# A scan and an MLP on one NeuronCore: dense idle products, copied states and other queues in the first scan

## The chip, the cores and the metric

The kernel runs on one core of a Trainium2 chip. The time is the device time of one execution in microseconds (us), as a median over runs. The engines are named as in the profile: PE (TensorE; PEld is its weight loading), DVE (VectorE), ACT (ScalarE), POOL (GpSimd) and SP (SyncE, which here only issues DMAs). A "q" after the name of an engine means its queue of DMA issues.

## What is computed

The first part is a state-space scan over 4 batches and 8 heads of 768 steps, in chunks, with state size N = 16 and head size D = 32. The second is an MLP on 3072 tokens with a quick GELU. The scan's output, with its heads side by side, is the MLP's input.

```python
log_a = np.log(np.clip(a, 1e-06, 1.0))
state = zeros((batch, H, N, D))
for c in range(nc):                      # chunks of the sequence
    cum = np.cumsum(la, axis=-1)         # la, xc, Bc, Cc: the chunk's parts
    L = np.exp(cum[:, :, :, None] - cum[:, :, None, :]) * causal
    M = np.einsum('bhin,bhjn->bhij', Cc, Bc) * L
    y_intra = np.einsum('bhij,bhjd->bhid', M, xc)
    y_inter = np.einsum('bhin,bhnd->bhid', Cc, state) * np.exp(cum)[:, :, :, None]
    y[:, :, sl] = y_intra + y_inter
    Bx = np.einsum('bhjn,bhjd->bhjnd', Bc, xc) * decay_from_j
    state = decay_full * state + np.sum(Bx, axis=2)
x = y.transpose(0, 2, 1, 3).reshape(3072, 256)
h = x @ w_in                             # 256 x 2048, float64 weights
out = (h * (1 / (1 + exp(-1.702 * h)))) @ w_out   # 2048 x 256
```

## The kernel before

**Tiling.** The 3072 tokens are cut into six groups of 512 tokens (`NG` groups of `TG`). A group has two pairs (`PG` = 2), a pair has two tiles of 128 tokens, and a tile has two chunks of 64. For each group the scan of its two pairs gives `yT`, the transposed input of the MLP. The MLP has 16 blocks of 128 hidden units; block f needs the weight columns f of `w_in`. Groups 0 and part of group 1 use plain products; in the later ones a product of 2 by 2 blocks is done with seven block products instead of eight (`first` for the hidden layer, `product` for the output).

**Order.** Every engine works through its instructions in the order in which the program's text issues them; `in_order` at the end pins that order. The scan of one group stands in between the products of the group before, so that PE always has products. Group 0 has nothing before it: its scan is the first thing that runs, and PE is then only partly occupied. This first scan is what the change touches.

**The first scan**, by its lines in the profile:

- `rows a` and the logarithm: SP and ACT load `az` (L274), DVE clips it (L339), ACT takes the logarithm (L341), and DVE forms the running sum `cum` inside each chunk (L343).
- `load_first` (L134) loads C and B of group 0 in four DMAs each, `fetch` (L180) loads a piece of the weights, and `load` (L150) loads x (and, for later pairs, b and c) in two DMAs for each of them. Before the change C goes through SP's queue, and B half through ACT's and half through SP's. Then the queue of SP has weight piece 0, x of pairs 0 and 1, and b and c of pair 2.
- `keep_busy` and `pads` (L438, L430) are idle products of PE on a tile of ones; nobody reads what they give. A pad is a product of 32 x 32; `keep_busy` gives products of 192 columns on the whole array.
- `mask_banks` (L546) fills PSUM with the causal mask, `differ_of` (L552) adds the differences of `cum`, and `decay_exp` (L573) takes the exponential on ACT: L.
- `turn_first` (L613) transposes C and B on DVE. `mask_blocks` (L655, ACT) and `mask_first` (L646, POOL) spread a pair's C over its heads. `turn_back` (L625) turns B back on PE for the increments. `score` (L678) multiplies C and B.
- `fields` (L192, L195), `clamp` (L203, L204), `rounded` (L208) and `join` (L219, L225) turn a piece of float64 weights, read as 32-bit words, into float32: `fields`, `rounded` and `join` on DVE, `clamp` on ACT. `narrow(i)` is `rounded(i)`, `fields(i + 1)` and `join(i)`. Pieces 0 to 3 hold two blocks of `w_in` each, pieces 4 and 5 hold four.
- `ends_first` (L466) weights B with the decay to the end of its chunk, `weigh` (L689) multiplies L with the scores, `gain` (L709) gives the increments A of the states, and `since_first` (L510, L515) the decays since a chunk's start.
- `parts_first` (L728) copies A into the tile `steps`, `drops` (L520) sets out the decays, and `keep_first` (L733) runs one scan over `steps`, which leaves the states of all chunks in it. In this tile the elements of one state lie eight elements apart.
- `finish`: `intra` (L814) and `inter` (L802) form y on PE, and two copies (L839, ACT) bring it to `yT`. `table` loads ACT's function table ahead of need. Then come the hidden products of group 0 (L868), first for f = 0.

PSUM has one area of four banks (`area`) which the scores and y take in turn, and four single banks (`bank`) taken in rotation. So y begins when both weighings have read the scores.

`fetch(1, held=True)` writes one word of its tile on DVE, and its DMA waits for that write. In the text it stands behind `weigh(0)`; pieces 2 to 5 and the rest of `a` follow it in SP's queue. After `join(1)` come `fetch(6)` and the load of pair 2's x.

**Later lines.** In group 1 some products are issued in two or four column pieces: `hidden` (L868) and `product` (L1029) cut the first ones, by a number written in the code.

Of the kernel before, what the change touches and what calls it, by code (L numbers as in the profile page):

```python
# [8 lines left out]
FP32 = mybir.dt.float32  # L9
# [7 lines left out]
P = 128  # L17
# [18 lines left out]
def kernel(  # L36
# [31 lines left out]
    nc = tc.nc  # L68
# [17 lines left out]
    R = 4  # L86
# [195 lines left out]
        nc.scalar.activation(early, early, f)  # L282

    table(AF.Ln)
    load_first("C", [nc.sync] * R)
    load_first("B", [nc.scalar] * 2 + [nc.sync] * 2)
    fetch(0)
    load(0, "x")
    load(1, "x")
    load(PG, "bc")  # L290


    edge = const.tile([P, 2], FP32, name="edge")
# [34 lines left out]

    idents = const.tile([P, 2 * NH, H], FP32, name="idents")

    def fold_ident(k):

        nc.vector.tensor_tensor(
            out=idents[:, k * NH:(k + 1) * NH],
            in0=ident[:, :H].unsqueeze(1).to_broadcast([P, NH, H]),
            in1=ident[:, H:].unsqueeze(1).to_broadcast([P, NH, H]), op=ALU.add)
# [393 lines left out]
    def keep_first():  # L730

        flat_steps = steps.rearrange("p e m -> p (e m)")
        nc.vector.tensor_tensor_scan(  # L733
            out=flat_steps, data0=drop.rearrange("p e m -> p (e m)"), data1=flat_steps,
            initial=0.0, op0=ALU.mult, op1=ALU.add)
        for p in range(PG):
            state[p] = steps.rearrange("p e m -> p m e")[:, 4 * p:4 * p + 4]

    def keep_both(pairs):

# [34 lines left out]
    def finish(pairs, steps=range(2)):  # L775


        g, first = divmod(pairs[0], PG)
        early = pairs[0] < PG
        if 0 in steps:  # L780
            begun_y[pairs[0]] = area(f"y{pairs[0]}")[:, :, :len(pairs) * 2 * H].rearrange(
                "p (s t) (k i) -> p s t k i", s=2, i=H), set()
        both, begun = begun_y[pairs[0]]
        y = [both[:, i] for i in range(2)]

        def begin(i, t, parts):
            new = not begun & {(i, t, q) for q in parts}
            begun.update((i, t, q) for q in parts)
            return new

        def inter(n, p, sides=range(2)):

            for k in range(2):
                for i in sides:
                    m = 2 * k + i
                    if (4 * p + m) % (2 * NC) == 0:
                        continue
                    old = state[p][:, m - 1] if m else state[p - 1][:, 3]
                    for r in range(R):
                        t = r // 2  # L800
                        rows, to = slice(32 * r, 32 * r + 32), Q * D * (r % 2)
                        nc.tensor.matmul(  # L802
                            out=y[i][to:to + Q * D, t, 2 * n + k], lhsT=old[rows],
                            rhs=st[p]["CsT"][rows, k, SIDES[i]],
                            start=begin(i, t, range(Q * (r % 2), Q * (r % 2) + Q)), stop=early,
                            tile_position=(32 * r, to), skip_group_check=True)

        def intra(n, p):
            L = Ls[p]
            for k in range(2):  # L810
                for h in range(NH):
                    t, q = divmod(h, HB)
                    for i, side in enumerate(SIDES):
                        nc.tensor.matmul(  # L814
                            out=y[i][D * q:D * q + D, t, 2 * n + k], lhsT=rx[p][side, k, h],
                            rhs=L[side, k, h // Q, h % Q],
                            start=begin(i, t, (q,)), stop=not early, tile_position=(H * i, D * q),
                            skip_group_check=True)

        cols = slice(2 * first * P, 2 * (first + len(pairs)) * P)  # L820

        if first == 0:
            yT[g] = ffn.tile([P, NK, TG], FP32, tag="yT", name=f"yT{g}")
        if early:
            for n, p in enumerate(pairs):
                intra(n, p)
            for i in range(2):
                for n, p in enumerate(pairs):
                    inter(n, p, (i,))
        else:  # L830
            for step in steps:
                for n, p in enumerate(pairs):
                    (inter, intra)[step](n, p)
            if 1 not in steps:
                return
        for i in range(2):
            o = yT[g][:, :, cols].rearrange("p t (k s i) -> p s t k i", s=2, i=H)
            if early:
                nc.scalar.activation(o[:, :, i], both[:, :, i], AF.Copy)  # L839
            else:  # L840
                nc.scalar.activation(o[:, i], y[i], AF.Copy)  # L841
        for p in pairs:
            state.pop(p - 1, None)
            st.pop(p)
            Ls.pop(p)
# [11 lines left out]
    def hidden(g, f):  # L857
        j, i = divmod(f, 2)
        if i == 0:
            block(g, j)  # L860
        h = bank(f"h{g}_{f}")
        for k in range(NK):
            n = 2 if g == 1 and NK * f + k < 14 else 1
            if n == 2 and NK * f + k < 14 - 8:
                n = 4
            for e in range(n):
                cols = slice(e * TG // n, (e + 1) * TG // n)
                nc.tensor.matmul(out=h[:, cols], lhsT=w_in[:, f, k], rhs=yT[g][:, k, cols],  # L868
                                 start=(k == 0 and e == 0), stop=(k == NK - 1),
                                 skip_group_check=True)  # L870

        nc.scalar.activation(gT[g, j][:, i], h, AF.Silu, scale=GELU_SCALE)
# [127 lines left out]
    def product(g, j, only=ORDER, ks=range(2)):  # L1000
# [22 lines left out]
        for i in only:  # L1023
            w, h = terms[i]
            if g < NG - 1:
                n = 2 if g == 1 and 7 * j + ORDER.index(i) < 5 else 1
                for k in range(n):
                    cols = slice(k * HT // n, (k + 1) * HT // n)
                    nc.tensor.matmul(out=acc[g][0][i][:, cols], lhsT=w, rhs=h[:, cols],  # L1029
                                     start=(j == 0 and k == 0 and (i, 0) in begins),  # L1030
                                     stop=(j == NF // 2 - 1), skip_group_check=True)
                continue
# [100 lines left out]
        differ(p, [(r, ab[p, r]) for r in range(R)])  # L1133

    busy = bank("busy")
    keep_busy(4, 45)
    both = area("ab0")
    for r in range(R):
        mask_banks(0, r, both[:, r])
    for r in range(R):  # L1140
        if r == R - 1:
            pads(11, busy)
        mask_banks(1, r, bank(f"ab1_{r}"))
    turn_first("C")
    turn_first("B")
    fold_ident(1)
    differ_of(0)
    decay_exp(0, None, both[:, :, :2 * Q * H])
    differ_of(1)
    mask_blocks(0)  # L1150
    mask_first(1)
    for r in range(R):
        decay_exp(1, r, ab[1, r])
    fields(0)
    rounded(0)
    clamp(0)
    score(range(PG), turn_back)
    ends_first(0)
    ends_first(1)
    since_first()  # L1160
    weigh(0)
    fetch(1, held=True)
    for i in range(2, 6):
# [5 lines left out]
    parts_first()  # L1169
    for p in range(PG):  # L1170
        since_start(p, nc.gpsimd)
    keep_first()
    table(AF.Silu)
    finish(range(PG))
    join(0)
    fields(1)
    clamp(1)
# [1 line left out]
    fields(2)  # L1179
    clamp(2)  # L1180
    join(1)
    load(PG, "x")


    def at(places, i, *work):
# [229 lines left out]
```

## Time and profile before

| What | Value |
|---|---|
| Median of 3 runs | 355.42 us (354.2 to 355.69) |
| The profiled execution | 354.92 us |
| Its span | 353.2 us |
| PE busy | 345.5 us, 98% of the span |
| DVE busy | 254.7 us, 72% |
| ACT busy | 149.0 us, 42% |
| POOL busy | 12.1 us, 3% |
| Mean granted clock of PE | 0.99 |
| First hidden product (L868) starts | 20.54 us into the span |

The profile is of one execution. Its page gives the busy time of each engine, the span in 40 slices (8.83 us each), the granted clock in tenths, and the costliest groups. Answers of the trace give more: the timeline (start, time, engine, line, operation, output and input tiles, count, and in brackets the idle time before and what ended it), and busy time by windows. In float32 one product of the program shows as two passes on PE, each with its weight load.

### The profile page before, as it was taken

How to read it: one execution, taken by the hardware profiler on the slowest of the kernel's cores; microseconds unless marked ns; L12 is line 12 of the kernel's file. 1: busy time of each engine (PE TensorE's matmuls, PEld its weight loads, DVE VectorE, ACT ScalarE, POOL GpSimd, SP SyncE). 2: the span in 40 equal slices, each digit the busy share in tenths (PEclk: the TensorE clock that was granted, in tenths of full speed). 3: DMA queues.
4: the chain of work that ended last, by engine and by line, in shares of the span. 5: the costliest groups of instructions: out<-in, count | busy, mean ns of one | idle time of the engine just before them, and what ended most of it. 6: DMA issues, size and time to landing. Idle time of an engine off the chain costs nothing.

```text
span 353.2 us, 8361 instructions
## 1 busy us (share of the span) xinstructions
PE 345.5 (98%) x3514; PEld 277.2 (78%) x3514; DVE 254.7 (72%) x481; ACT 149.0 (42%) x332; POOL 12.1 (3%) x40
## 2 busy tenths in 40 slices
PE   8699999999999999999999999999999999999996
PEld 7554444456989888888888888888888888889996
DVE  5859997999967999667898466788474555465463
ACT  3848657004363431754423554333554331553320
POOL 7200000100000100000000000000000000000000
PEclk9969999999999999999999999999999999999999
DMA  4899599562534400416614016400000200000301
GB/s 109 129 303 298 171 191 237 95 82 48 106 64 101 94 0 2 74 43 125 113 27 73 0 41 127 84 8 2 1 4 2 46 15 1 0 2 0 61 0 60
DMA packets 89982, 25.93 MB, mean 73 GB/s; under 512 B 73433, under 2 KB 87129, under 8 KB 89945
## 3 DMA queue, kind: packets, MB, share of 16 engines
q1 hardware_dynamic: 89272, 25.02, 32.9%
q8 instruction: 27, 0.44, 0.5%
q10 hardware_dynamic: 672, 0.39, 0.4%
q14 instruction: 11, 0.08, 0.1%
HBM read 22.15 MB, written 3.24 MB: 72 GB/s over the span
## 4 chain that ended last, share of the span: by engine, by line
PE 96%; DVE 2%; ACT 1%; issue 1%; DVEq 0%
PE acc L1029 28%; PE X L924 18%; PE Y L934 14%; PE h L868 11%; PE o L966 8%; PE acc L1036 7%; PE y L814 3%; PE y L802 2%; PE cb L678 2%; PE A L709 1%; PE busy L438 1%; DVE L L689 1%; PE busy L430 1%; PE ab L546 0%; PE ab L552 0%
## 5 line engine op out<-in xcount | busy, mean ns | idle before, releaser
L929 ACT ACTIVATE ac<-X 128x256 f32<-128x256 f32 x76 | 29.0, 382 | 79.0 <-PE X L924 78.6
L1029 PE MATMUL acc<-mg,mw 128*128 128x256 f32 (+1 forms) x196 | 54.6, 375 | 0.0
L901 ACT ACTIVATE gT<-gT 128x512 f32<-128x512 f32 (+1 forms) x76 | 39.3, 520 | 33.1 <-DVE gT L1056 32.4
L1056 DVE TENSOR_TENSOR gT<-Y,ac 128x512 f32<-128x512 f32 x38 | 26.2, 689 | 36.8 <-PE Y L934 29.9
L924 PE MATMUL X<-my,mi 128*128 128x256 f32 x152 | 45.1, 379 | 0.0
L1056 DVE TENSOR_TENSOR gT<-Y,b 128x256 f32<-128x256 f32 x38 | 15.8, 419 | 34.5 <-PE Y L934 34.5
L1029 PEld LDWEIGHTS acc<-mg,mw 128*128 128x128 f32 x196 | 36.8, 191 | 4.8
L868 PE MATMUL h<-yT,w_in 128*128 128x512 f32 (+2 forms) x120 | 38.6, 482 | 0.7 <-ACT yT L839 0.7
L1029 PE MATMUL acc<-gT,w_out 128*128 128x256 f32 (+1 forms) x132 | 35.6, 373 | 0.0
L868 PEld LDWEIGHTS h<-yT,w_in 128*128 128x128 f32 x120 | 20.1, 201 | 17.9 <-issue 15.7
L924 PEld LDWEIGHTS X<-my,mi 128*128 128x128 f32 x152 | 28.0, 190 | 3.5
L966 PE MATMUL o<-gT,w_out 128*128 128x512 f32 x64 | 28.6, 597 | 0.0
L892 DVE TENSOR_TENSOR mg<-gT 128x512 f32<-128x512 f32 x40 | 27.2, 681 | 0.0
L1029 PEld LDWEIGHTS acc<-gT,w_out 128*128 128x128 f32 x132 | 24.6, 190 | 3.3 <-ACT yT L841 0.2
L929 ACT ACTIVATE b<-X 128x256 f32<-128x256 f32 x38 | 14.6, 383 | 20.5 <-PE X L924 20.1
L924 PE MATMUL X<-yT,w_in 128*128 128x256 f32 x76 | 23.2, 389 | 0.0
L934 PE MATMUL Y<-my,mi 128*128 128x256 f32 x76 | 22.7, 381 | 0.1
L934 PE MATMUL Y<-yT,w_in 128*128 128x256 f32 x76 | 22.7, 381 | 0.0
L934 PE MATMUL Y<-yT,mi 128*128 128x256 f32 x76 | 22.5, 380 | 0.0
L924 PE MATMUL X<-my,w_in 128*128 128x256 f32 x76 | 22.5, 380 | 0.0
L966 PEld LDWEIGHTS o<-gT,w_out 128*128 128x128 f32 x64 | 11.8, 190 | 13.2 <-issue 12.8
L400 DVE TENSOR_TENSOR_SCAN L<-a,idents 128x1024 f32<-128x1024 f32 x9 | 20.5, 2276 | 0.0
(153 smaller groups left out, 543.2 us busy)
## 6 DMA issues: line engine op xcount, KB each, us to landing
a<-scratch SPq DMA_DIRECT2D x18, 256.0 KB, 5.0
bits<-in_moe_w_out_dram SPq DMA_DIRECT2D x8, 512.0 KB, 6.8
x<-in_x_dram SPq DMA_DIRECT2D x24, 128.0 KB, 3.3
out_dram<-ob SPq DMA_DIRECT2D x40, 64.0 KB, 1.9
bits<-in_moe_w_in_dram SPq DMA_DIRECT2D x8, 256.0 KB, 3.8
bits<-in_moe_w_in_dram SPq DMA_DIRECT2D x4, 512.0 KB, 8.2
b<-in_B_dram SPq DMA_DIRECT2D x20, 64.0 KB, 2.6
af<-in_a_dram SPq DMA_DIRECT2D x3, 384.0 KB
```

The costliest lines, as they stand in the source:

```text
L400: nc.vector.tensor_tensor_scan(out=L, data0=ra[p].rearrange("p k e -> p (k e)"), data1=idents.rearrange("p h i -> p (h i)"), initial=0.0, ...
L814: nc.tensor.matmul(out=y[i][D * q:D * q + D, t, 2 * n + k], lhsT=rx[p][side, k, h], rhs=L[side, k, h // Q, h % Q], start=begin(i, t, (q,)) ...
L868: nc.tensor.matmul(out=h[:, cols], lhsT=w_in[:, f, k], rhs=yT[g][:, k, cols], start=(k == 0 and e == 0), stop=(k == NK - 1), skip_group_ch ...
L892: nc.vector.tensor_tensor(out=t[:, 0:2], in0=B[:, :, 1], in1=B[:, 0], op=ALU.subtract)
L901: nc.scalar.activation(o, i, AF.Silu, scale=GELU_SCALE)
L924: nc.tensor.matmul(out=s["X"], lhsT=lhsT, rhs=rhs, start=i == "1", stop=i == "4", skip_group_check=True)
L929: nc.scalar.activation(copy, s["X"], AF.Copy)
L934: nc.tensor.matmul(out=o, lhsT=lhsT, rhs=rhs, start=s.pop("new", False), stop=i != "5", skip_group_check=True)
L966: nc.tensor.matmul(out=o[c], lhsT=w_out[:, c, f], rhs=gT[g, f // 2][:, f % 2], start=(f == 0), stop=(f == NF - 1), skip_group_check=True)
L1029: nc.tensor.matmul(out=acc[g][0][i][:, cols], lhsT=w, rhs=h[:, cols], start=(j == 0 and k == 0 and (i, 0) in begins), stop=(j == NF // 2 - ...
L1036: nc.tensor.matmul(out=o[k] if type(o) is list else o[:, cols], lhsT=h[:, cols], rhs=w, start=(j == 0 and (i, k) in begins), stop=(j == NF ...
L1056: nc.vector.tensor_tensor(out=o, in0=v, in1=w, op=ALU.add)
```

## The change

- `load_first("C")` goes wholly through ACT's queue, `load_first("B")` wholly through SP's.
- The load of pair 2's b and c leaves its place ahead of weight pieces 1 to 5; after `join(1)` pair 2 is loaded whole (`load(PG)`: b, c, x).
- `keep_busy(4, 45)` becomes `keep_busy(5, 0)`, and the 11 pads ahead of the last mask are left out. A new function `dense(n)` issues n idle products of 256 columns on the whole array. One stands ahead of `finish`, one between `intra` and `inter`, and one after `finish`.
- The mask of C for pair 0 moves from ACT to POOL, that for pair 1 from POOL to ACT, behind the exponentials of pair 1.
- `turn_back` moves ahead of `score`, and `since_first` takes its place between the two pairs' scores. On DVE `rounded(0)` moves behind `ends_first`; on ACT `clamp(0)` moves behind `parts_first`.
- `fold_ident(1)` moves from DVE to POOL, behind `keep_first`.
- `keep_first` copies the states of the two pairs out of `steps` into two tiles of their own, one on DVE and one on POOL; `inter` then reads those.
- In group 1 fewer products are cut: in `hidden` the first 3 in four and the next 5 in two, in place of 6 and 2; in `product` none, in place of 5 in two.

```diff
-    load_first("C", [nc.sync] * R)
-    load_first("B", [nc.scalar] * 2 + [nc.sync] * 2)
+    load_first("C", [nc.scalar] * R)
+    load_first("B", [nc.sync] * R)
     fetch(0)
     load(0, "x")
     load(1, "x")
-    load(PG, "bc")
...
-    def fold_ident(k):
+    def fold_ident(k, engine=nc.vector):
-        nc.vector.tensor_tensor(
+        engine.tensor_tensor(
...
-        for p in range(PG):
-            state[p] = steps.rearrange("p e m -> p m e")[:, 4 * p:4 * p + 4]
+        for p, copy in zip(range(PG), (nc.vector.tensor_copy, nc.gpsimd.tensor_copy)):
+            state[p] = ssd.tile([P, 4, Q * D], FP32, tag="S", name=f"S{p}", bufs=3)
+            copy(state[p], steps.rearrange("p e m -> p m e")[:, 4 * p:4 * p + 4])
...
             for n, p in enumerate(pairs):
                 intra(n, p)
+            dense(1)
             for i in range(2):
...
-            n = 2 if g == 1 and NK * f + k < 14 else 1
-            if n == 2 and NK * f + k < 14 - 8:
+            n = 2 if g == 1 and NK * f + k < 11 else 1
+            if n == 2 and NK * f + k < 11 - 8:
                 n = 4
...
-                n = 2 if g == 1 and 7 * j + ORDER.index(i) < 5 else 1
+                n = 2 if g == 1 and 7 * j + ORDER.index(i) < 0 else 1
...
     busy = bank("busy")
-    keep_busy(4, 45)
+    def dense(n):
+        if n:
+            t = bank("dense")
+        for i in range(n):
+            nc.tensor.matmul(out=t[:, :4 * H], lhsT=ones,
+                             rhs=ones[:, :H].unsqueeze(1).to_broadcast([P, 4, H]),
+                             start=True, stop=True, skip_group_check=True)
+
+    keep_busy(5, 0)
     both = area("ab0")
     for r in range(R):
         mask_banks(0, r, both[:, r])
     for r in range(R):
         if r == R - 1:
-            pads(11, busy)
+            pads(0, busy)
         mask_banks(1, r, bank(f"ab1_{r}"))
     turn_first("C")
     turn_first("B")
-    fold_ident(1)
     differ_of(0)
     decay_exp(0, None, both[:, :, :2 * Q * H])
     differ_of(1)
-    mask_blocks(0)
-    mask_first(1)
+    mask_first(0)
     for r in range(R):
         decay_exp(1, r, ab[1, r])
+    mask_blocks(1)
+    turn_back()
     fields(0)
-    rounded(0)
-    clamp(0)
-    score(range(PG), turn_back)
     ends_first(0)
     ends_first(1)
-    since_first()
+    rounded(0)
+    score(range(PG), since_first)
     weigh(0)
     fetch(1, held=True)
...
+    clamp(0)
     keep_first()
+    fold_ident(1, nc.gpsimd)
     table(AF.Silu)
+    dense(1)
     finish(range(PG))
+    dense(1)
     join(0)
...
     join(1)
-    load(PG, "x")
+    load(PG)
```

## The prediction

> **What bounds the kernel now.** I read the page first, for who is busy and at which clock.
>
> ```profile
> span 353.2 us, 8361 instructions
> PE 345.5 (98%) x3514; PEld 277.2 (78%) x3514; DVE 254.7 (72%) x481; ACT 149.0 (42%) x332; POOL 12.1 (3%) x40
> PEclk9969999999999999999999999999999999999999
> ```
>
> TensorE (PE) is busy for 98% of the span, so after the first scan only PE work counts. One slice of the clock row, the third (17.7 to 26.5 us), stands at 6. The second view is busy time and clock by windows (columns: the window, its length, busy time and count of PE, weight loads, DVE, ACT, POOL, then clock, DMA share, GB/s):
>
> ```profile
> 18.00:19.90 1.90, 1.82 (x56) 1.68 (x56) 0.40 (x1) 0.01 (x1) 0.00 (x0) 1.00 0.98 282
> 19.90:21.00 1.10, 0.46 (x1) 0.46 (x2) 0.76 (x2) 1.10 (x3) 0.00 (x0) 0.50 0.90 247
> 23.30:26.70 3.40, 3.40 (x6) 1.34 (x5) 2.98 (x7) 1.93 (x3) 0.00 (x0) 0.50 1.04 341
> 26.70:30.00 3.30, 3.30 (x9) 1.53 (x8) 3.27 (x7) 2.63 (x5) 0.00 (x0) 0.99 1.10 370
> ```
>
> From 19.9 to 26.7 the clock is half, just as the first hidden products begin. The timeline of weight loads shows their spacing:
>
> ```profile
> 24.96 0.34 PEld L868 LDWEIGHTS h<-yT,w_in 128*128 128x128 f32 x1 [0.52 <-issue]
> 25.82 0.34 PEld L868 LDWEIGHTS h<-yT,w_in 128*128 128x128 f32 x1 [0.52 <-issue]
> 27.14 0.19 PEld L868 LDWEIGHTS h<-yT,w_in 128*128 128x128 f32 x1 [0.24 <-issue]
> 27.57 0.19 PEld L868 LDWEIGHTS h<-yT,w_in 128*128 128x128 f32 x1 [0.24 <-issue]
> ```
>
> 0.855 us apart cold, 0.43 warm. About seven products run cold: 7 x 0.425 = **3.0 us lost**. The other loss is the wait before them, in the timeline of all engines:
>
> ```profile
> 12.76 2.35 DVE L689 TENSOR_TENSOR L<-L,cb 128x1024 f32<-128x1024 f32 x2
> 15.26 1.37 PE L814 MATMUL y<-L,x 64*32 64x64 f32 x117 [0.96 <-DVE L L689]
> 15.87 1.22 DVE L733 TENSOR_TENSOR_SCAN steps<-drop,steps 128x512 f32<-128x512 f32 x1
> 17.65 0.33 PE L814 MATMUL y<-L,x 64*32 64x64 f32 x11 [1.02 <-issue]
> 17.91 1.91 PE L802 MATMUL y<-CsT,steps 32*64 32x64 f32 x56
> 19.89 1.08 ACT L839 ACTIVATE yT<-y 128x512 f32<-128x512 f32 x2 [2.70 <-PE y L802]
> 20.54 1.22 PE L868 MATMUL h<-yT,w_in 128*128 128x512 f32 x1 [0.72 <-ACT yT L839]
> ```
>
> PE waits for DVE's weighting (to 15.11), stops 1.02 us for nothing shown, then forms y from the strided running sum. From 20.54 on PE has no gap over 0.15 us until its end. And SyncE's queue, which carries weights:
>
> ```profile
> 7.25 3.63 SPq L150 DMA_DIRECT2D x<-in_x_dram  x4
> 10.93 2.34 SPq L150 DMA_DIRECT2D b<-in_B_dram  x2
> 13.31 1.62 SPq L150 DMA_DIRECT2D c<-in_C_dram  x2
> 15.04 8.70 SPq L180 DMA_DIRECT2D bits<-in_moe_w_in_dram  x10
> ```
>
> The b and c of the next pair stand ahead of weight pieces 1 to 5, and DVE waits for piece 1 until 20.21 and for piece 2 until 23.68.
>
> [...]
>
> **The change part by part.** All times are on this trace's clock.
>
> *Start of PE.* 45 + 11 small pads go (1.66 + 0.38 us); a fifth 192-column product comes. Eight passes took 2.93, so ten take 3.66: 1.21 to 4.87. Eight masks (seven took 1.29) add 1.47, to 6.34. The cumulative sum is ready at 5.61, so the differences start at 6.4 instead of 7.41, 1.0 earlier.
>
> *C from ACT, B from SP.* C's four issues leave SP; ACT's two took 1.26, so four end near 4.4, before ACT's logarithm at 4.47, which stands behind them and which everything awaits. [...] I take 0, bound 0 to 0.5. SP reaches piece 0 about 1.0 earlier, so its fields start near 9.4 instead of 10.44. The transpose of B ends near 8.7 instead of 9.09.
>
> *Masks.* The first moves to POOL (1.04 there, free from 7.9): ready at 9.0 instead of 10.64. ACT does the four exponentials of pair 1 (9.0 to 10.1) and then the second mask (0.90, to 11.0). turn_back now needs only B and a free bank: 9.4 to 10.0. Score 0 ends at 10.6, rows 11.3, score 1 11.9, where the old one ended at 12.6.
>
> *DVE.* fold_ident (0.67) leaves. Fields 0.77 from 9.4, ends 0.76 and rounded 0.69 end at 11.6; both weighings (2.35) at 14.0 against 15.11. drops 0.71 and scan 1.22: 15.9 against 17.09. **Gain 1.1 us.**
>
> *Copies of the states, added.* DVE's: drops moves 448 elements in 0.71, so 256 take about 0.41, to 16.3. POOL's: 128x256 with two inputs took 0.71 (1.42 for two), so I take 0.7. [...] Bounds of the net effect: later groups of 56 L802 products from contiguous states took 0.97 to 1.10 us in the chain, this one 1.91, so 0.8 comes back against 0.4 to 1.1 paid. y then ends near 17.8 instead of 19.82. clamp(0) (1.48) moves behind ACT's parts, and the Silu table (1.28 + 0.20) behind it. The last products of A waited for x at 13.95; with SP about 0.8 earlier they end near 13.4, the parts (1.28) near 14.8, so the table is in by 17.8. That is just in time; 0 to 0.3 late. POOL's fold (1.04, by its equal-shaped mask) runs beside join(0) and may hold it up by its length; join(0) then ends at 18.6 at worst, when first wanted. The hidden products start about **2.0 us earlier** (18.7 of 20.7 effective; bounds 1.0 to 2.6).
>
> *Three dense products*, each two passes of 256 columns at 0.215, 0.43 us. They lie in waits: 0.96 before y, the wait for the states, 0.72 before h. Free there; 0.43 each if the cover is gone, and perhaps 0.2 is paid at the second. Their worth is the clock[...]. Bounds: 0 (still cold) to 3.0 (never cold). I take 3.0, since products of the earlier stages, no denser, kept full clock.
>
> *b and c behind the weights.* Their two and two issues (2.34 + 1.62) go from before piece 1. Piece 1 then waits for the held DVE memset behind the first weighing (12.8) instead of SP; SP's slow issue at 15.04 (1.58 for one) was behind b and c. Piece 1 lands near 16.5, and piece 2 near 19.5, 4 us earlier. Their cost comes after fetch(6): four more issues at up to 1.9 each end before b is first read (44.2) and mostly before SP's store of a (37.1). 0, bound 0 to 0.5.
>
> *Who is late next.* Warm from 18.7, f=2 comes at 18.7 + 8 x 0.43 = 22.1. join(1) ended at 25.77, now near 21.9. f=8 comes at 32.4; join(4) ended at 36.26 and moves 4 us, to 32.3. Both fit narrowly; I charge 0.2.
>
> *Splits.* 6 fewer pieces in h and 5 in acc. Four unsplit h products take 3.43, the split groups 3.57 and 3.71, or 0.02 a piece; acc's two split products 0.93 against 0.86, 0.035 a piece. Together 0.25.
>
> *Instruction refills.* The page has 27 instruction packets for some 7030 PE instructions, about 260 each; the 1.02 us stop amid y looks like one that came late. The pads were 224 instructions. The stop probably stays, near 15.1 to 16.1, under the wait for the scan: 0, bound 0 to 0.8.
>
> Sum: 2.0 + 3.0 + 0.25 - 0.2 = 5.05 us from the profiled execution's own 354.92 (span 353.2 and 1.7 around it): 349.9. The median, 355.42, stands 0.5 above it, so **350.3 us**.
>
> **Rivals.** *Still cold* (chance 0.20): [...] For: the window before 19.9 was 68% busy and still lost the clock. Only start and splits: 355.4 - 2.25 = 353.1. *Weights bind* (0.12): piece 2 lands only 1.5 us earlier, near 22.1, join(1) ends at 24.3, f=2 starts 2.8 earlier instead of 5.0: 352.4. For: DMA engines are 0.9 to 1.1 busy from 18 to 30. Against: they moved 70 GB/s or less from 15 to 17. *Nothing comes* (0.07): POOL's copy is slow, the table is late and the clock stays low; 354.9. *Slower* (0.06): refills. All later bursts of small products (about 20) meet refills at other places, since 252 instructions less are issued. Each late one costs 1.0; against a gain of 5.05, it takes seven or more to be slower than now by more than 0.5%; with eight 350.3 + 8 = 358.3. [...] That the idle products aren't issued at all is excluded by the program's order, which has them.
>
> **How the numbers follow.** The likeliest, 0.55, is 350.3. Its own range is 348.8 to 351.6 from the bounds of start and copies. To reach the cold case with its spread, the range goes up to 353.6; nothing-comes and slower stay out (0.13), with the low tail. A measurement here can tell 0.5%, 1.78 us, from no change: faster 0.55 + 0.20 + 0.12 = 0.87, same 0.07, slower 0.06.
>
> **What would show it.** Right: no clock of 0.50 after the first warm-up; L868 spaced 0.43 from its first product, near 18.7; the L802 group near 1.0; weighing done at 14.0; DVE's wait for piece 2 gone by 19.5. The forecast is wrong if h starts later than 19.7, if the cold stretch is still there, if PE waits for join(1) or join(4), or if new gaps called issue stand in later bursts.

## The result, and the profile after

The changed kernel takes **351.78 us** (median of 4 runs, 351.27 to 352.25), the kernel before in the same measurement 355.50 (4 runs, 354.2 to 355.69): ratio 0.9903, interval 0.9874 to 0.9932. That is faster by about 3.7 us. A second measurement gave 352.32 (10 runs) against 355.0 (21 runs): 0.9922 (0.9894 to 0.9949). The prediction was 350.3 in a range of 348.8 to 353.6. The sign and the range hold, and both parts of the mechanism, an earlier start and a full clock, are in the trace; 1.5 us of the forecast gain did not come. The profiled execution, the fastest of the four, took 351.27 with a span of 349.3, so 2.0 us lie around the span (1.7 before).

The page, with utilization and the clock row:

```profile
span 349.3 us, 8110 instructions
PE 341.4 (98%) x3388; PEld 272.9 (78%) x3388; DVE 255.8 (73%) x481; ACT 149.2 (43%) x332; POOL 14.5 (4%) x42
PEclk9999999999999999999999999999999999999999
```

The 6 in the third slice is gone. Work by windows (columns as before: window, length, then busy time and count of PE, weight loads, DVE, ACT, POOL; clock, DMA share, GB/s):

```profile
16.20:17.46 1.26, 1.22 (x57) 1.10 (x57) 1.23 (x2) 0.00 (x0) 1.26 (x2) 1.00 0.98 311
17.46:18.94 1.48, 0.63 (x2) 0.23 (x2) 1.48 (x2) 1.09 (x2) 1.06 (x2) 1.00 0.87 264
18.94:22.40 3.46, 3.43 (x8) 1.47 (x9) 3.39 (x8) 3.14 (x5) 0.00 (x0) 1.00 0.94 287
29.30:33.26 3.96, 3.65 (x10) 1.36 (x8) 3.81 (x5) 3.17 (x5) 0.00 (x0) 1.00 0.83 174
```

The clock is 1.00 throughout. Look at the other columns too: DVE is now busy in nearly all of each window, and in the last one PE is not (3.65 of 3.96). The timeline of weight loads gives the spacing of the first hidden products, 0.43 from the start:

```profile
19.48 0.19 PEld L869 LDWEIGHTS h<-yT,w_in 128*128 128x128 f32 x1 [0.24 <-issue]
19.91 0.19 PEld L869 LDWEIGHTS h<-yT,w_in 128*128 128x128 f32 x1 [0.24 <-issue]
```

The timeline of all engines through the end of the first scan (start, time, engine, line, operation, tiles, count, and in brackets the idle time and who ended it):

```profile
11.34 2.37 DVE L688 TENSOR_TENSOR L<-L,cb 128x1024 f32<-128x1024 f32 x2 [0.52 <-PE cb L677]
...
13.86 1.47 PE L814 MATMUL y<-L,x 64*32 64x64 f32 x128 [1.20 <-DVE L L688]
14.44 1.23 DVE L732 TENSOR_TENSOR_SCAN steps<-drop,steps 128x512 f32<-128x512 f32 x1
...
15.70 0.39 DVE L737 COPY S<-steps 128x256 f32<-128x256 f32 x1
15.73 0.86 POOL L737 COPY S<-steps 128x256 f32<-128x256 f32 x1 [3.21 <-DVE steps L732]
...
16.01 1.14 DVE L219 SCALAR_TENSOR_TENSOR p<-bits,p 128x512 uint32<-128x512 uint32 x1
...
16.24 1.22 PE L802 MATMUL y<-CsT,S 32*64 32x64 f32 x56 [0.28 <-DVE S L737]
16.56 1.71 POOL L332 TENSOR_TENSOR idents<-ident 128x512 f32<-128x512 f32 x1
17.18 1.64 DVE L225 SCALAR_TENSOR_TENSOR w_in<-m,p 128x512 f32<-128x512 f32 x1
...
17.53 1.09 ACT L840 ACTIVATE yT<-y 128x512 f32<-128x512 f32 x2 [1.46 <-PE y L802]
...
18.97 4.53 PE L869 MATMUL h<-yT,w_in 128*128 128x512 f32 x10 [0.88 <-DVE w_in L225]
```

Weighing ends at 13.71 (15.11 before). y is formed without a stop in it (1.02 before), L802 takes 1.22 instead of 1.91, and h starts at 18.97 instead of 20.54. But h no longer waits for ACT's `yT`: it waits for DVE's `join(0)`, whose two instructions (L219, L225) take 1.14 and 1.64 here, each beside a POOL instruction. Before, with POOL idle, they took 0.67 and 0.69:

```profile
17.01 0.67 DVE L219 SCALAR_TENSOR_TENSOR p<-bits,p 128x512 uint32<-128x512 uint32 x1
17.71 0.69 DVE L225 SCALAR_TENSOR_TENSOR w_in<-m,p 128x512 f32<-128x512 f32 x1
```

SP's queue carries the weights from 12.60, with b and c of pair 2 now behind them:

```profile
12.60 7.46 SPq L180 DMA_DIRECT2D bits<-in_moe_w_in_dram  x10
20.11 4.09 SPq L269 DMA_DIRECT2D az<-in_a_dram  x4
24.29 1.33 SPq L180 DMA_DIRECT2D bits<-in_moe_w_out_dram  x2
27.64 3.17 SPq L150 DMA_DIRECT2D b<-in_B_dram  x2
```

New are the waits around f = 8, in the timeline again:

```profile
29.42 0.69 DVE L192 TENSOR_SCALAR p<-bits 128x1024 uint32<-128x1024 uint32 x1 [0.30 <-DMA bits<-in_moe_w_in_dram]
...
31.89 1.23 DVE L225 SCALAR_TENSOR_TENSOR w_in<-m,p 128x1024 f32<-128x1024 f32 x1
...
33.26 1.96 PE L869 MATMUL h<-yT,w_in 128*128 128x512 f32 x4 [0.32 <-DVE w_in L225]
```

DVE's `fields(5)` waits 0.30 for weight piece 5, which lands at 29.30. Four instructions of DVE later (3.7 us) `join(4)` gives the blocks 8 to 11, and PE has waited 0.32. The chain that ended last passes, between 14 and 34 us, through the load of piece 5 and DVE's work on it:

```profile
18.29 11.01 DMA bits<-in_moe_w_in_dram
...
30.72 1.15 DVE p L219
```

Ahead of that load stand SP's ten issues of weights, from 12.60 on, behind the held write at 12.51.

Later there is one more PE wait of this kind, 0.28 us at 86.2, for DVE (L458). Before it, DVE waited 0.96 us for the last piece of `w_out`, which landed at 55.07.

A table of both profiles, and of those experiments that are used below for it, splits each span at the same instructions. The columns are the start of the first hidden product (h0), from there to f = 8, to the end of group 0's hidden products, to the first product at L925, and to the end; then the cold time of PE that touches this stretch (cold: at a granted clock of 0.50):

```text
kernel                    h0     to f8   to f15  to L925  to end  cold
before                    20.54  16.90   15.45   42.33    257.97  6.8
after                     18.97  14.29   15.53   42.56    257.91  -
after again               19.50  14.78   15.53   42.91    258.12  -
e3 no dense               19.37  15.42   15.45   42.12    258.14  3.4
e5 no copies              18.90  14.74   15.53   43.76    257.91  -
e13 all early             20.70  13.91   15.53   42.13   258.06  -
e15 after, two blocks     19.36  13.81   15.45   42.79    257.90  -
e16 before, two blocks    21.26  13.84   15.45   42.54    257.99  -
```

### The profile page after: what moved, and what is told of

It reads as the page before. It is cut to its first block, busy times and chain, and to the rows that moved or that the text cites. A ratio compares the mean times of both kernels' runs of the same rounds, so it can differ in the third digit from the quotient of the medians.

```text
span 349.3 us, 8110 instructions
## 1 busy us (share of the span) xinstructions
PE 341.4 (98%) x3388; PEld 272.9 (78%) x3388; DVE 255.8 (73%) x481; ACT 149.2 (43%) x332; POOL 14.5 (4%) x42
## 4 chain that ended last, share of the span: by engine, by line
PE 75%; DMA 9%; DVE 8%; SPq 5%; issue 2%; ACT 0%; ACTq 0%; DVEq 0%
PE acc L1030 28%; PE X L925 19%; PE Y L935 14%; PE acc L1037 7%; DMA a<-scratch 4%; DMA bits<-in_moe_w_in_dram 3%; PE cb L677 2%; PE y L814 2%; SPq L180 2%; SPq L124 1%; DVE L L399 1%; PE y L802 1%; PE h L869 1%; DVE p L219 1%; SPq L150 1%
## 5 line engine op out<-in xcount | busy, mean ns | idle before, releaser
L1030 PE MATMUL acc<-mg,mw 128*128 128x256 f32 x192 | 54.5, 379 | 0.0
L925 PE MATMUL X<-my,mi 128*128 128x256 f32 x152 | 45.1, 379 | 0.0
L1057 DVE TENSOR_TENSOR gT<-Y,b 128x256 f32<-128x256 f32 x38 | 15.9, 420 | 34.8 <-PE Y L935 34.8
L869 PE MATMUL h<-yT,w_in 128*128 128x512 f32 (+2 forms) x108 | 35.6, 485 | 1.2 <-DVE w_in L225 1.2
L1030 PE MATMUL acc<-gT,w_out 128*128 128x256 f32 x128 | 35.5, 379 | 0.0
L869 PEld LDWEIGHTS h<-yT,w_in 128*128 128x128 f32 x108 | 18.2, 190 | 17.4 <-issue 13.6
L925 PEld LDWEIGHTS X<-my,mi 128*128 128x128 f32 x152 | 28.0, 190 | 3.7
L925 PE MATMUL X<-yT,w_in 128*128 128x256 f32 x76 | 23.2, 389 | 0.0
L925 PE MATMUL X<-my,w_in 128*128 128x256 f32 x76 | 22.5, 379 | 0.0
```

Source lines behind the costliest of these rows:

```text
L925: nc.tensor.matmul(out=s["X"], lhsT=lhsT, rhs=rhs, start=i == "1", stop=i == "4", skip_group_check=True)
L1057: nc.vector.tensor_tensor(out=o, in0=v, in1=w, op=ALU.add)
```

## The experiments

All are timed against the kernel before on the same chip; its medians there were 355.0 us (after again, e1, e3, e6), 354.52 (e4, e8, e12, e13) and 354.69 (e5, e15, e16, e18). The intervals of the ratios are about 0.2 to 0.35% to either side, so differences under some 1 us between two experiments are read from the profiles, not from the times. A profile is one execution, so a part of a column above may differ by some tenths from run to run.

### The changed kernel again

> The changed kernel once more, as the measure for the others on this chip: 351.8 us, ratio 0.990. All theories expect the same. In its trace: no clock of 0.50 after the warm-up, the first hidden product near 19.0, join(0)'s two DVE instructions near 1.1 and 1.6 us, PE waiting about 0.3 us each before f=2 and f=8.

352.32 us (350.62 to 353.99, 10 runs), all ten at full clock (0.999 to 1.0). In its profile the first hidden product starts at 19.50 and not at 18.97, piece 5 lands at 30.30 instead of 29.30, DVE waits 0.73 instead of 0.30 for it, and PE's wait before f = 8 is 0.81 instead of 0.32. So the place of the new wait is stable, and its size goes with the landing of piece 5. The wait before f = 2 that was expected is in neither profile.

### e1: the fold back on DVE

```diff
     turn_first("B")
+    fold_ident(1)
...
     keep_first()
-    fold_ident(1, nc.gpsimd)
```

> The changed kernel with fold_ident(1) back on DVE behind the transposes. Theory [...]: join(0)'s two instructions fall back from 1.14 and 1.64 to 0.67 and 0.69, hidden products start at 18.5 to 18.9 instead of 18.97, the wait before f=2 goes; but f=8 still waits for join(4), which waits for piece 5 landing at 29.3, so the total moves by less than 0.4: 351.4 to 351.9. Rival 1 (join(0) is slow for another reason[...]): both stay over 1 us. Rival 2 (DVE's length of work bounds f=8, not the landing): f=8 starts 0.5 to 1 earlier and the total falls to 350.9.

352.24 us, ratio 0.9915 (0.9887 to 0.9944). DVE and POOL in its timeline:

```profile
16.29 0.87 POOL L737 COPY S<-steps 128x256 f32<-128x256 f32 x1 [3.21 <-DVE steps L732]
16.56 1.14 DVE L219 SCALAR_TENSOR_TENSOR p<-bits,p 128x512 uint32<-128x512 uint32 x1
...
17.74 0.69 DVE L225 SCALAR_TENSOR_TENSOR w_in<-m,p 128x512 f32<-128x512 f32 x1
```

Without POOL's fold beside it, L225 is back at 0.69 from 1.64; L219, still beside POOL's copy, stays at 1.14. h0 came 4.47 after the end of weighing (14.26), where the changed kernel needed 5.26. The time did not change: f = 8 starts at 33.75, since DVE waited 0.78 for piece 5 and PE then 1.01 for DVE, and near 66 us PE waited another 0.96 for DVE.

### e3 and e4: the dense products alone

e3 is the changed kernel without them:

```diff
-            dense(1)
             for i in range(2):
...
-    dense(1)
     finish(range(PG))
-    dense(1)
```

> The changed kernel without the three dense products in the waits; those at the start stay. Theory (they hold the clock): a stretch of 0.50 from about 17 to 24 us comes back, the hidden products stand 0.85 apart there, and 3.0 us are lost, less the 0.6 that PE now waits for weights: 353.9 to 354.5. Rival (the shorter scan alone keeps the clock): no 0.50, 351.4 to 351.8.

352.9 us, ratio 0.9926 (0.9901 to 0.995). Mean clocks were 0.99 or 0.995 in all ten runs, where the changed kernel on that chip had full clock in all ten. One cold stretch of 3.41 us, at 0.50, lowers the mean over 351 us by 0.005, so there were one or two. **In this kernel the dense products hold the clock.** In the profile it was one:

```profile
15.80:19.21 3.41, 1.36 (x73) 1.02 (x56) 3.34 (x5) 2.19 (x4) 2.79 (x3) 1.00 0.94 302
19.21:22.62 3.41, 3.25 (x4) 1.51 (x5) 3.34 (x9) 2.81 (x4) 0.00 (x0) 0.50 0.95 276
```

PE was busy 1.36 of the 3.41 us ahead of it, and lost the clock. Yet f = 8 starts at 34.79, only 0.5 later than in the repeat of the changed kernel (34.28). The cold stretch made PE late at f = 2 by 1.5 us (24.49 against 23.01), and 1.0 of it came back, because in the repeat PE waits 0.81 before f = 8, and here, where `join(4)` ends at 33.13, it doesn't. The spans end at 350.5 and 350.8. By the medians the time is 0.6 us above the repeat's, inside the intervals; the expected 353.9 or more did not come.

e4 puts the same three products into the kernel before.

```diff
                 intra(n, p)
+            dense(1)
             for i in range(2):
...
+    dense(1)
     finish(range(PG))
+    dense(1)
```

> The kernel before with the three dense products added in the same three waits and nothing else. Prediction's step: the clock is worth 3.0 us, so 352.0. Theory now (PE, once warm, only runs into DVE's chain of weight conversion): the clock holds, but f=2 waits for join(1), which ends at 25.77 whatever PE does, and f=8 for join(4) at 36.25, so f=8 starts at 36.4 instead of 37.44: about 1.0 us faster, 354.0. Rival: the clock drops all the same, 355.0.

354.26 us (22 runs), ratio 1.0002 (0.998 to 1.0024): no gain. 12 of 22 runs were at full clock (8 of 75 of the kernel before there); their median is 354.05, that of the eight 353.50. The profile fell on one of the slowest runs, 356.73, and shows a stop in y:

```profile
16.19 1.35 PE L814 MATMUL y<-L,x 64*32 64x64 f32 x115 [0.61 <-DVE L L689]
20.84 0.46 PE L814 MATMUL y<-L,x 64*32 64x64 f32 x13 [3.30 <-issue]
```

The stop that the prediction met as 1.02 us is 3.30 here. One 16 KB packet of instructions is fetched between 18.0 and 19.7, in the middle of it, while the weights' queue (q1) alone takes 95.9% of the DMA engines' time. With the added products the place of the stop moves too: y stops behind 115 of its products, and not behind 117. In this profile the longer stop takes more than the clock could give, and the clock is at 0.50 again from 18.94 to 25.76. Only two of the 22 runs have a mean clock as low as this one's 0.99, so what took the gain in the others is not shown.

### e6: b and c of pair 2 ahead of the weights again

```diff
     load(1, "x")
+    load(PG, "bc")
...
     join(1)
-    load(PG)
+    load(PG, "x")
```

> The changed kernel with the load of pair 2's b and c back ahead of the weight pieces. Theory (weights bind once the clock holds): piece 1 lands 2 to 3 us later than 16.8 and piece 5 later than 29.3, PE waits before f=2 for join(1) and before f=8 for join(4), total 353.5 to 354.5. Rival (the place of b and c is immaterial since the held write opens piece 1): 351.6 to 352.1.

352.26 us, ratio 0.992 (0.9892 to 0.9949). Piece 1 lands at 19.82 instead of 16.79, and PE waits for it ahead of f = 2:

```profile
23.96 1.53 PE L870 MATMUL h<-yT,w_in 128*128 128x512 f32 x3 [0.94 <-DVE w_in L225]
```

That is nearly a microsecond, but f = 8 starts at 34.46, only 0.18 later than in the repeat of the changed kernel, where PE had to wait there. The first theory's 353.5 or more was missed, and so was its wait at f = 8. Piece 5 lands at 29.79, between the 29.30 and 30.30 of the two profiles of the changed kernel: in these profiles the place of b and c decides when piece 1 lands, not when piece 5 does.

### e8, e12 and e13: the weights earlier

e8 issues pieces 1 to 5 and the rest of `a` right behind x, with no held write, and does POOL's fold right after its mask. e12 puts the load of pair 3 behind the fetch of the last weights. e13 has both. In the diff below, the changes of `at` are those of e12, all that stands above them is e8.

```diff
     load(1, "x")
+    fetch(1)
+    for i in range(2, 6):
+        fetch(i)
+    rows_a(az, (nc.sync,))
...
-    fetch(1, held=True)
-    for i in range(2, 6):
-        fetch(i)
-    rows_a(az, (nc.sync,))
...
     mask_first(0)
+    fold_ident(1, nc.gpsimd)
...
-    fold_ident(1, nc.gpsimd)
...
-    at(in_hidden[0], 5, store_a, lambda: fetch(7), lambda: fetch(8),
-       lambda: load(PG + 1))
+    at(in_hidden[0], 5, store_a, lambda: fetch(7), lambda: fetch(8))
...
+    at(in_hidden[0], 6, lambda: load(PG + 1))
```

> The changed kernel with the weight pieces 1 to 5 and the rest of a issued right behind x, with no held write, and with fold_ident(1) on POOL right behind the first mask. Theory (f=8 waits for join(4), bound by the landing of piece 5 and by 1.4 us of DVE lost to POOL's fold): piece 5 lands 2 to 3 us earlier (26 to 27), join(0) takes 0.67 + 0.69, join(4) ends near 31.7, no wait at f=2 or f=8, block 15 of the hidden products ends 1.0 us earlier than in the changed kernel. If a later wait, for w_out's last piece and the scan of pair 3 behind it on DVE, binds as well, less than half of that reaches the end: 351.3 to 351.8; if not, 350.8.

e8: 352.95 us, ratio 0.9947 (0.9924 to 0.9971), no faster than the changed kernel. 7 of its 22 runs are at full clock, with a median of 351.99; the profile fell on a run of 354.32 with two cold stretches of 3.41 us. In it piece 5 lands at 25.78, 3.5 us earlier, and both halves of the early weights' price stand in PE's timeline:

```profile
14.62 1.16 PE L818 MATMUL y<-L,x 64*32 64x64 f32 x97 [1.19 <-DVE L L692]
18.23 0.68 PE L818 MATMUL y<-L,x 64*32 64x64 f32 x31 [2.46 <-issue]
18.84 1.22 PE L1145 MATMUL dense<-ones 128*128 128x256 f32 x2
```

The packet of instructions, fetched between 16.0 and 17.0, now meets weight traffic (q1 takes 94.3% of the DMA engines' time from 15.9 to 17.1), and with the 2.46 us stop the clock is lost as well (0.50 from 16.56 to 23.39) in spite of the dense products. h0 is 22.71. Nor is DVE helped: it waits 3.60 us for ACT's `clamp(1)`, which stands in ACT's order behind the copies of the late y, and `join(4)` ends at 36.22, not near 31.7.

> The changed kernel with the load of pair 3 (b, c, x) behind fetch(9) in SP's queue. Theory (the last piece of w_out lands at 55 us, DVE waits 1 us for it and is then busy without a pause until the increments at 86, for which PE waits 0.3): piece 9 is issued near 39 instead of 47.7 and lands before 52, the DVE wait and PE's wait near 86 go, total 0.3 to 0.6 us less than the changed kernel on this chip. Rival (nothing after f=8 binds): no change in the total.

e12: 351.54 us (22 runs), ratio 0.9927 (0.9909 to 0.9945). The last piece of `w_out` lands at 48.17 instead of 55.07, DVE's wait for it and PE's near 86 are gone (DVE waits 0.8 for a load of `a`, L477, instead), and the time cannot be told from the changed kernel's.

> Both of the last two together. Theory (two meeting points of PE with DVE and the weights, f=8 near 33 us and the increments near 86, take what the prediction gave to the clock and the start): PE has no wait over 0.2 us after its first hidden product, which starts near 18.7, and the total is 1.3 us under the changed kernel, 350.3. Rival (only DVE's length of work binds, not landings): half of that.

e13: 353.18 us, ratio 0.9952 (0.9925 to 0.9978). In its profile the stop in y is 0.81, one stretch is cold (16.38 to 19.80) and h0 is 20.70, not 18.7. Behind h0 PE waits for nobody, as expected, and from there to the end it needs 329.63, where the kernel before needs 332.66. The expected 350.3 was missed; its four runs at full clock have a median of 351.45, no better than e12.

### e15 and e16: no waiting for weights in group 0

```diff
-                nc.tensor.matmul(out=h[:, cols], lhsT=w_in[:, f, k], rhs=yT[g][:, k, cols],
+                nc.tensor.matmul(out=h[:, cols], lhsT=w_in[:, f if g else f % 2, k],
+                                 rhs=yT[g][:, k, cols],
```

e15 is the changed kernel with this edit, e16 the kernel before.

> The changed kernel, but the hidden products of group 0 read block f modulo 2 of w_in (weight piece 0) instead of block f, so group 0's hidden products wait for no later weight piece (this leaves out the right weights in group 0). Theory A (PE, once warm, meets the weight conversion of pieces 1 to 5 on DVE, and about a microsecond of the gain is lost there): no gap of PE before f=2 and f=8, f=8 starts near 32.5 instead of 33.3 to 34.3, and the time is 350.5 to 351.3, 0.7 to 1.5 under the changed kernel. Theory B (the full-clock gain was lost further on, at the output weights and DVE, whatever happens at f=2 and f=8): f=8 is earlier as well, but the time stays within 0.4 of the changed kernel (351.8 to 352.3).

e15: 350.85 us (350.33 to 352.05, 6 runs), ratio 0.99 (0.9869 to 0.9931). In its timeline sixteen hidden products run through f = 8 (33.17) with no wait:

```profile
28.45 7.03 PE L869 MATMUL h<-yT,w_in 128*128 128x512 f32 x16
```

From h0 to f = 8 it needs 13.81, so the changed kernel loses 0.48 there and its repeat 0.97. But in this profile piece 5 landed at 28.45, DVE did not wait for it, and `join(4)` ended at 33.10: the right weights would have been there in time too, so the profile gives PE's pace without a wait and not the worth of the edit. The time lies in theory A's interval, but the ratio does not separate it from the changed kernel (0.9903 and 0.9922). The loss at f = 8 is shown by the profiles, not by the times.

> The kernel before, with the same edit: group 0's hidden products read block f modulo 2 of w_in (this leaves out the right weights in group 0). The two cold windows still cost PE about 3 us at f=8. Theory A (the cold windows were partly free because PE waited for DVE's conversion anyway): before had hardly a wait to lose while cold, so its profile stays within 0.5 of 355, and the difference to the same edit of the changed kernel grows from 3.5 to between 4 and 5 us. Theory B (lost further on): the difference between the two edited kernels stays at 3 to 3.7.

e16: 354.57 us (352.83 to 357.49, 22 runs), ratio 1.0008 (0.9985 to 1.0032). By the medians, it is 3.72 us above e15, at the upper edge of theory B. Its profile fell on the fastest run, which was at full clock, and this is what the prediction needed:

```profile
21.20:28.20 7.00, 6.94 (x16) 3.15 (x17) 5.25 (x10) 6.17 (x11) 0.00 (x0) 1.00 0.90 283
```

With the same instructions from h0 to f = 8, warm takes 13.84 and cold (before) 16.90. The difference is **3.06 us**: the clock term's size. Among its runs two cold stretches of 3.41 us cost less than that: nine runs with a mean clock near 0.99 (two stretches) have a median of 355.33, the five at full clock 353.36, a difference of 2.0. The profile at full clock starts h at 21.26, 0.72 later than the profile before, which would make up most of the gap; whether a late start and a kept clock go together in general was not tried.

### e5: the states read from the running sum

```diff
-        for p, copy in zip(range(PG), (nc.vector.tensor_copy, nc.gpsimd.tensor_copy)):
-            state[p] = ssd.tile([P, 4, Q * D], FP32, tag="S", name=f"S{p}", bufs=3)
-            copy(state[p], steps.rearrange("p e m -> p m e")[:, 4 * p:4 * p + 4])
+        for p in range(PG):
+            state[p] = steps.rearrange("p e m -> p m e")[:, 4 * p:4 * p + 4]
```

> The changed kernel without the two copies of the states: inter reads them strided from the running sum, as before. By the prediction's step: the L802 group takes 1.9 instead of 1.22 but starts about 0.4 to 0.6 earlier, so the first hidden product comes 0 to 0.4 later (18.9 to 19.4); join(0)'s first instruction falls to 0.67 since POOL's copy is gone from beside it. Time: within 0.4 of the changed kernel if PE meets DVE's conversion after it anyway (351.6 to 352.4); 352.5 or more if contiguous states matter to the end.

351.88 us (12 runs), ratio 0.9926 (0.9903 to 0.9949): no difference. The timeline is instructive:

```profile
16.01 0.67 DVE L219 SCALAR_TENSOR_TENSOR p<-bits,p 128x512 uint32<-128x512 uint32 x1
16.27 1.91 PE L801 MATMUL y<-CsT,steps 32*64 32x64 f32 x56
...
16.72 0.69 DVE L225 SCALAR_TENSOR_TENSOR w_in<-m,p 128x512 f32<-128x512 f32 x1
...
18.90 1.12 PE L868 MATMUL h<-yT,w_in 128*128 128x512 f32 x2
```

y is 0.69 slower (1.91 against 1.22) but `join(0)` is done at 17.41 instead of 18.82, since POOL has no copy to wait for and does the fold at 12.87, beside the weighing. Measured from the end of weighing, y ends 4.08 us later here and 3.75 in the changed kernel, so the copies bring 0.33. The first hidden product comes 4.80 later here and 5.26 there, so **the copies and what they do to `join(0)` cost 0.46**.

### e18: two repairs together

The changed kernel with POOL's fold right after its first mask, as in e8, and pair 3's load late, as in e12; the held write stays.

> The changed kernel with two moves: POOL's fold of the identity right behind its first mask (out of the way of join(0)), and the load of pair 3 behind the fetch of weight piece 9. Theory A [...]: join(0)'s second instruction 0.69 instead of 1.64, piece 9 lands near 48, no DVE wait there, first hidden product near 18.7, time 351.0 to 351.6. Theory B (DVE's own chain binds whatever comes earlier): these moves are seen in the trace but the time is 351.6 to 352.3, like the changed kernel's.

351.42 us (350.6 to 353.38, 8 runs), ratio 0.9913 (0.9879 to 0.9947). L225 is at 0.69 and the wait for `w_out` is gone, as forecast. h0 is not: 19.74, with half clock from 14.74 to 18.16.

```profile
14.73 2.04 PE L814 MATMUL y<-L,x 64*32 64x64 f32 x128 [1.84 <-DVE L L688]
16.71 1.22 PE L1141 MATMUL dense<-ones 128*128 128x256 f32 x2
```

PE had stood idle for 1.84 us, DVE being later (weighing ends at 14.59), and here the first dense product was not enough. The ratio is not told apart from the changed kernel's, and no other version was shown to be better than it.

## Why the prediction was right or wrong

The forecast gain was 5.05 us on the profiled execution; it is 3.65 (354.92 to 351.27), or 3.9 in the span. Step by step:

**Start, 2.0 forecast, 1.57 measured (1.04 in the repeat).** The forecast's own h0 of 18.7 is 1.84 before 20.54; the 2.0 counts from an "effective" 20.7 that no line shows. The times up to the states were right or too careful: differences at 5.62 (forecast 6.4), weighing done at 13.71 (14.0), the scan at 15.67 (15.9), y at 17.46 (17.8). In the repeat they are some 0.5 later (6.17, 14.25, 16.20, 18.00), from the weighing on up to 0.3 behind the forecast. C's four issues on ACT didn't move the logarithm (4.42; before 4.47): they ended at 4.19, though twice the 1.26 of the old two, from 2.23 on, would have been 4.75 and not the 4.4 of the forecast. The end of `join(0)` was put at 18.6 "at worst, when first wanted"; it ended at 18.82, and h waited for it. The term "POOL's fold may hold it up by its length" was right in kind, but POOL's copy of the states holds up the first half of `join(0)` too (0.47), and the fold itself took 1.71 beside DVE, not 1.04. e1 and e5 show that DVE's two instructions are longer beside POOL's: 1.64 against 0.69, 1.14 against 0.67. How POOL's lengthen them, no run shows.

**Clock, 3.0 forecast, 3.06 by e16's profile.** The seven products times 0.425 were right. That three dense products would be enough to keep the clock was the author's estimate, and e3 shows that in this kernel they are what holds it. The cold stretches of the profiles are 3.41 or 6.83 us long, to 0.01. The rival "still cold" is out for this kernel: all 14 runs of the changed kernel kept the clock, none of e3's ten, and 16 of the 131 of the kernel before in the experiments. With the same three products e8, e13 and e18 lose it behind a stop of 0.8 to 2.5 us or an idle time of 1.8. In time this term is worth less than 3.0: 0.6 by the medians of e3 and the repeat, inside the intervals, and 1.4 to 2.0 by the runs of the kernel before (see the end of this section).

**Splits, 0.25 forecast** (6 x 0.02 and 5 x 0.035 add to 0.30). From f = 15 to L925 the kernel before takes 42.33 with no wait. The best of those with the new splits take 42.12, so 0.2. Behind L925 nothing is seen (257.97 and 257.91).

**Who is late next, 0.2 forecast: the step that failed.** After h0 the changed kernel should have saved 3.0 + 0.25 - 0.2 = 3.05; it saved 2.37 (332.66 to 330.29), and in the repeat 1.32 (331.34). The prediction had f = 8 at 32.4 and `join(4)` at 32.3, and called that narrow but enough. It gave `join(4)` the 4 us that it expected of piece 2, and dated no landing of piece 5. Piece 5 landed at 29.30, only 2.3 earlier than before (31.58), while piece 1 came 3.3 earlier (16.79, from 20.12); the DMA engines show a mean busy share of 0.87 to 1.10 from 17.5 to 29.3. `join(4)` ended at 33.11, 3.14 earlier, and at 34.14 in the repeat.

The loss is 0.48 at f = 8 (0.97 in the repeat), and it is the landing that makes it. In the profiles in which DVE doesn't wait for piece 5 (before, e3, e4, e6, e8, e13, e15), `join(4)` ends 4.73 to 4.78 behind the end of `join(3)`; in the changed kernel it is 5.13, and 5.58 in the repeat. Without that wait, an estimate from these figures, `join(4)` would have ended at 32.72, and PE, at its 13.81 from h0, have come at 32.78. Of the profiles with the change, just those in which DVE waits for piece 5 (0.30, repeat 0.73, e1 0.78, e5 0.24, e12 0.09) have a wait of PE before f = 8 (0.32, 0.81, 1.01, 0.74, 0.12). From f = 15 to L925 the loss is 0.4 (0.8), of which the wait near 86 is 0.28 (0.34). That second wait was not in the prediction at all. A wait for `join(4)` was among its signs of being wrong. Its rival "weights bind" was wrong where it stood (`join(1)` ended at 22.25, not 24.3) and right in kind one meeting later.

This is also why single parts are worth so little. Before, PE needed 16.90 us to f = 8 and DVE kept up; now PE could be there in 13.8, and DVE is busy for 17.3 of the 17.9 us from 15.4 to 33.3, where before it was for 16.4 of 20.4. So an earlier landing alone could give the 0.4 us of the estimate above (0.8 in the repeat), and then DVE's own length binds (the first line is before, the second after):

```profile
17.00:37.44 20.44, 19.07 (x100) 9.26 (x99) 16.36 (x29) 13.75 (x21) 0.00 (x0) 0.83 0.89 264
15.40:33.26 17.86, 16.38 (x93) 7.43 (x93) 17.32 (x27) 13.88 (x21) 2.79 (x3) 1.00 0.97 270
```

e1 (h0 earlier), e3 (a cold stretch), e5 (no copies) and e6 (piece 1 late) change h0 or f = 2 by 0.2 to 1.5 us and the time by nothing that could be measured with certainty. What is early at h0 or f = 2 is given back where PE waits at f = 8; e8 and e13, which come to h0 late, keep 2.89 and 3.03 of the 3.05 behind it. By these profiles the whole change brings the move of DVE's chain, `join(4)` 2 to 3 us earlier, with PE warm enough to follow; no experiment moved that chain alone.

**The stop in y, forecast to stay, went.** In the changed kernel the packet of instructions is fetched between 12.4 and 13.4, before y begins, and until 13.5 the DMA engines move nothing else. The prediction said that a stop would cost nothing, under the wait for the scan. In the changed kernel there is none to judge by; in the profiles of e4 and e8 it cost 3.30 and 2.46.

**The rival "slower by refills"** was wrong for this kernel: no stop of that kind over 0.15 us is in its two profiles after the start. But such stops do come later than y: one is 0.94 us near 80.5 in e5, 0.56 near 81.4 in e1 and 0.41 near 80.5 in e18, each named "issue". All stops of this kind, in y and near 81, come at the same places of PE's instruction stream, as the last section shows. The changed kernel passes these places too, and its packets are there in time.

**Still open.** The difference of 2.0 us (e16) and 1.4 us (the kernel before, 354.96 for 56 runs with two cold stretches against 353.55 for 16 at full clock) between runs by their clock is under the 3.06 of the profiles. A late start in the runs that keep the clock would explain it; the one profile of such a run fits, and that is not enough to show it.

## What to carry to other kernels

When a cold or late engine is sped up, date the next supplier at every point where they meet (here f = 2, f = 8 and the last weights), from the last landing through each instruction behind it; a forecast margin of 0.1 us is none, since the landing alone differed by 1.0 between two profiles. Before work is given to POOL "for free", look at what DVE runs beside it: two idle-looking POOL instructions took 1.4 us out of the one DVE step that PE was waiting for. And look at what else is fetched while transfers that are moved earlier run: in e8 the packet of PE's instructions came amid the early weights, and PE stood still for 2.46 us.

## What the runs showed of the hardware

- PE's stops and the packets of instructions. In ten places of the profiles PE stands still with no other name than "issue", 0.25 (e12) to 3.30 us (e4), and it goes on 1.2 to 1.6 us after the end of a 16 KB packet of instructions (before: the packet from 14.90 to 16.12, PE from 17.65). Counted in PE's records (products and weight loads), 705, 961, 1729 or 1730 stand before such a stop, so the places lie 256 and 768 or 769 records apart; the kernel before has 27 packets of this size for 7028 records, 260 for each. In the changed kernel record 705 is passed at 14.8, 1.4 after the end of its packet (13.37), with no stop. In e4 and e8, amid weight traffic, the packet starts only when PE already stands (at 18.0 and 16.0, PE's last products ending at 17.54 and 15.78); but the stop in e5 near 80.5 comes with the DMA engines idle.
- The clock. The kernel before has full clock for 13.65 us (6.26 to 19.91), then half clock for 6.83; the second is half of the first, and a fourth of the first is 3.41, the length of the cold stretches of e3, e13 and e18. In the profiles the clock falls only at whole steps of 3.41 us from the start of the trace's first entry at full clock: four steps in the kernel before and in e3 (5.56 to 19.21), three in e4, e8, e13 and e18 (there 4.50 to 14.74). In the step before the fall PE was busy for 2.30 us (before), 1.36 (e3), 1.40 (e4), 1.44 (e8) and 1.53 (e13, e18), and at most one dense product, 0.70 us for its two passes, lies in it. The poorest step of the changed kernel has 2.21, that of its repeat 2.15, and they hold the clock. No threshold of busy time follows: e3 holds it behind a step with 1.86, and the kernel before loses it behind 2.30.
- POOL beside DVE. POOL's fold beside `join(0)` took 1.71 where POOL's mask of the same shape, with DVE at a transpose beside it, took 1.03, and the DVE instruction took 1.64 instead of 0.69.
